# Attention scores on half the rows of the array, the two heads in turn

## The chip, the core and the metric

The kernel runs on one core of a Trainium2 chip. The metric is the device time of the whole launch in microseconds (us), the median of several runs. The core's engines work side by side and each runs its own instructions in order: TensorE (PE; PEld in rows is its loading of weights), VectorE (DVE), ScalarE (ACT), GpSimd (POOL). SyncE (SP) issues the transfers (DMA) from and to memory. SBUF is the large memory on the chip with 128 partitions (rows); PSUM, in eight banks, is where TensorE writes.

## The reference, cut to what matters

```python
def _attn_ref(q, k, v, M_prev, z_prev, beta):          # B, H, S, D = 4, 8, 576, 64
    scores = q @ k^T / sqrt(D);  causal mask
    a = softmax(scores)
    local = a @ v
    q_p = where(q > 0, q, exp(q) - 1) + 1
    mem_out = (q_p @ M_prev) / (q_p . z_prev + 1e-6)
    g = sigmoid(beta)
    return g * mem_out + (1 - g) * local
# then, on the 2304 tokens with 512 channels:
#   h = x @ w_in; solu = h * softmax(h); layer norm * g_ln; @ w_out
#   sigmoid(x @ w_gate) * (x @ w_val) @ w_out
```

There are 32 heads (4 batches of 8) of 576 positions and 64 channels. The scores are causal, so a query needs only the keys up to its own position.

## The kernel before, in words

The program has three parts: attention, the first expert layer (`Moe1`) and the gated second one (`Moe2`). Only attention is changed.

Attention takes the heads in 16 pairs. A pair's q, k and features are transposed on TensorE (`trans`, line 265; tiles trq, trk, trf), so that channels lie on the partitions: head 0 on rows 0 to 63, head 1 on rows 64 to 127. For accuracy q and k are each split into a high and a low part (`tq_h`, `tq_l`, `tk_h`, `tk_l`: ScalarE writes the high part, VectorE the low one); a score is the sum of three products, q high by k high, q low by k high, q high by k low. Queries go in blocks of 128 (blocks 0 to 3) and a tail of 64 (block 4, where both heads' tails share the 128 columns of the weights and the 576 keys are cut in two halves). Block i needs 128 (i + 1) keys.

In `s_p` (line 352) q is the stationary operand and k the moving one. Both heads' k lie in one tile of 128 rows, so q is kept in a tile `q2` that has zeros in the rows of the other head: head 0's columns first, then the tails, then head 1's. GpSimd writes these zeros once at the start (line 185). Each matmul uses all 128 rows; the first head's three are issued, then the second's.

VectorE adds the mask and takes the row maxima (`s_m`, line 372), ScalarE the exponentials and their sums (`s_e`, line 380), GpSimd divides (`n_p`, line 389). The probabilities are transposed (`g_p`, `t_p`, `tt_p`, `tc_p`: tiles t..a, t..b, t..c, t..d) and copied to SBUF by ScalarE or VectorE. The products with v and with the memory (`x_m` line 444, `x_a` line 459; tile x) are f32 matmuls with 64 columns of weights, head 0 on the left columns of the array and head 1 on the right ones; each leaves two records in the trace. The share of the memory is computed beside it (`ph_e` to `ph_s`). In the gaps the first layer's weights are converted (`cv_*`).

Scores and the three transposes of q, k and features take turns in two PSUM buffers of two banks each (tag "s"); the transposed probabilities have two buffers of one bank, x two.

The order of all this is a table, `ORDER`: each entry names a step and the pair it works on, as an offset to the running index. `run` walks the table once per index, so it fixes the order on every engine. The steps around attention, among them the load gl (line 794) and its scaling on VectorE (line 795), are placed by a planner.

Of the kernel before, what the change touches and what calls it, by code (L numbers as in the profile page):

```python
# [9 lines left out]
F32R = mybir.dt.float32r  # L10
# [8 lines left out]


ORDER = """
n23_r:-1 s1_e:0 s4_m:0 tt_c:-1 tc_c:-1 s3_m:0 lk:1 cv_r:-1 n3_p:-1 s0_e:0 s4_e:0 x1_c:-2 a00:-2 g1_p:-1 tf_p:0
t3_p:-1 g1_c:-1 tf_c:0 n2_p:-1 t3_c:-1 x0_c:-2 s2_p:0 t2_p:-1 t0_p:-1 cv_b:-1 ph_e:1 t2_c:-1 n4_r:0 n01_r:0 tq_p:1
cv_p:-1 n1_p:0 lz:1 t0_c:-1 t1_p:-1 g0_p:-1 cv_h:-1 tq_h:1 s2_m:0 t1_c:-1 ph_m:1 tk_p:1 tk_h:1 x0_m:-1 x1_m:-1
a13:-1 tq_l:1 tk_l:1 ph_g:1 n0_p:0 n4_p:0 cv_d:1 lv:0 a12:-1 a11:-1 a14:-1 a10:-1 ph_r:1 lq:2 ph_s:1 s3_e:0 s2_e:0
a01:-1 s1_p:1 s0_p:1 s1_m:1 tt_p:0 s0_m:1 g0_c:-1 tc_p:0 s4_p:1 cv_l:-1 s3_p:1 cv_a:0
""".split()


# [6 lines left out]
def f32(ap):  # L36
    return ap.bitcast(F32)
# [13 lines left out]
def kernel(  # L51
# [16 lines left out]
    nc = tc.nc  # L68
    B, H, S, D = q.shape
# [3 lines left out]
    P = 128  # L73
    NB = S // P
    S0 = NB * P
    TL = S - S0
# [74 lines left out]
    class Attention:  # L151
        def __init__(self, sb, ps, xe):
            self.sb, self.ps = sb, ps
            hw = S // 2

            self.pr = [{} for _ in pairs]
            self.kt = [xe.tile([P, 10 * D], F32, tag="xs", name=f"kt{n}") for n in range(2)]
            self.zm = sb.tile([P, HP, P], F32, tag="zm", name="zm0", bufs=2)
            self.qt = [sb.tile([P, 10 * D], F32, tag=f"qt{n}", name=f"qt{n}") for n in range(2)]


            mask = sb.tile([P, 2 * S0], F32, tag="mask", name="mask")
            nc.gpsimd.memset(mask, 0.0)
            for m in (mask[:, S0 - P : S0], *(mask[r : r + 64, S0 + hw - TL : S0 + hw] for r in (0, 64))):
                nc.gpsimd.affine_select(
                    out=m, in_=m, pattern=[[-1, m.shape[1]]], compare_op=ALU.is_ge,
                    fill=-1e30, base=0, channel_multiplier=1,
                )
            self.mask = mask[:, :S0]
            self.maskt = mask.rearrange("p (j w) -> p j w", j=2)[:, :, :hw]  # L170


            tail = slice(8 * D, 10 * D)
            self.vt = [sb.tile([P, 10 * D], F32, tag=f"vt{n}", name=f"vt{n}") for n in range(3)]
            for t in (*self.kt, *self.qt, *self.vt):
                nc.vector.memset(t[64:128, tail], 0.0)
            self.p4, self.q2 = [], []
            for n in range(2):
                p4 = sb.tile([P, S + TL], F32, tag=f"p4{n}", name=f"p4{n}")
                nc.vector.memset(p4[:, S:], 0.0)  # L180
                self.p4.append(p4)

                q2 = sb.tile([P, 2, 2 * S], F32R, tag=f"q2{n}", name=f"q2{n}")
                for hh in range(2):
                    nc.gpsimd.memset(f32(q2[64 - 64 * hh : 128 - 64 * hh, :, hh * S : hh * S + S]), 0.0)
                self.q2.append(q2)
            self.mt = []
            for n in range(3):
                mt = sb.tile([P, 2, D], F32, tag=f"mt{n}", name=f"mt{n}")
                nc.vector.memset(mt, 0.0)  # L190
                self.mt.append(mt)
# [29 lines left out]
            return self.ps.tile(shape, F32, tag=tag, name=name, bufs=2)  # L221


        def load_qk(self, n, t, src):
            b, hp = pairs[n]
            for hh in range(2):
                nc.sync.dma_start(
                    t[:, : 8 * D].rearrange("p (c h d) -> p c h d", h=2, d=D)[:, :, hh],
                    src[b, 2 * hp + hh, :S0, :].rearrange("(c p) d -> p c d", p=P),
                )  # L230
            nc.sync.dma_start(
                t[0:64, 8 * D : 10 * D].rearrange("p (h d) -> p h d", h=2),
                src[b, 2 * hp : 2 * hp + 2, S0:, :].rearrange("h p d -> p h d"),
            )
# [2 lines left out]
            self.load_qk(n, self.qt[n % 2], q)  # L237

        def lk(self, n, r):
            self.load_qk(n, self.kt[n % 2], k)  # L240

        def lv(self, n, r):
            b, hp = pairs[n]
# [27 lines left out]

        def q_parts(self, n, r):

            for hh, src, dst in ((0, 0, 0), (1, 0, S + TL), (1, S0, S)):
                sl, w = slice(64 * hh, 64 * hh + 64), S if hh == 0 else S0 if src == 0 else TL
                yield r["qps"][sl, src : src + w], *(self.q2[n % 2][sl, c, dst : dst + w] for c in range(2))

        def tq_h(self, n, r):
# [59 lines left out]
        def s_p(self, n, r, i):  # L338
            ps = r["s", i] = self.psum([P, 2, 512], f"sc{n}_{i}")
            q2, kh, kl = self.q2[n % 2], r["kh"], r["kl"]  # L340
            for j in range(2):
                if i == NB:

                    ks, x = slice(j * S // 2, (j + 1) * S // 2), ps[:, j, : S // 2]
                    qs = [q2[:, c, S0 : S0 + P] for c in range(2)]
                else:
                    w = P * (i + 1)
                    ks, x = slice(0, w), ps[:, j, :w]
                    q0 = w - P + j * (S + TL)
                    qs = [q2[:, c, q0 : q0 + P] for c in range(2)]  # L350
                for m, (c, kk) in enumerate(((0, kh), (1, kh), (0, kl))):
                    nc.tensor.matmul(x, qs[c], kk[:, ks], start=m == 0, stop=m == 2)  # L352

        def parts(self, r, i):

# [444 lines left out]
    ps = ctx.enter_context(tc.tile_pool(name="ps", bufs=2, space=PSUM, reuse_waits="tile"))  # L800
# [51 lines left out]
```

## Time and profile before

| | us |
|---|---|
| median of three runs (915.29 to 916.43) | 916.21 |
| the profiled execution | 914.82 |
| its span, first to last instruction | 913.0 |
| TensorE busy | 888.3 (97%) |
| VectorE busy | 567.2 (62%) |
| ScalarE busy | 432.1 (47%) |
| GpSimd busy | 267.0 (29%) |

The busy shares are means over stages that differ. Attention fills the first 238 us and there VectorE and ScalarE are nearly as busy as TensorE; in the layers that follow TensorE alone is. A row of the list of instructions gives line, engine, operation, written tile <- read tiles, shapes, count, and busy time with the mean in ns. In the list by time the first number is the start, the second how long the group took; TensorE's instructions are pipelined, so their cost is read from start to start and not from the durations. An idle time before a group stands in brackets with what ended it.

### The profile page before, as it was taken

The page shows a single profiled execution, that of the slowest core. Times are in us where ns is not written, and L with a number is a line of the kernel's source. Part 1 is how long each engine was busy: PE and PEld are TensorE (multiplying, and loading weights), DVE is VectorE, ACT ScalarE, POOL GpSimd, SP SyncE. Part 2 cuts the span into 40 slices and gives each one's busy share as a digit, 9 for nine tenths or more (in the row PEclk, how much of TensorE's full clock was granted, in tenths as well). Part 3 has the DMA queues.
Part 4 walks back from the last instruction along what each step waited for, and adds up shares of the span by engine and source line. Part 5 has one row for each costly group of instructions (what it writes and reads, how often), then busy time and mean ns, then how long its engine had stood idle before and what let it go on. Part 6 is the DMA issues. An engine that isn't in the chain of part 4 may idle for free.

```text
span 913.0 us, 13960 instructions
## 1 busy us (share of the span) xinstructions
PE 888.3 (97%) x5224; PEld 753.2 (82%) x5224; DVE 567.2 (62%) x1321; ACT 432.1 (47%) x941; POOL 267.0 (29%) x322
## 2 busy tenths in 40 slices
PE   5899999999989999999999999999999999999998
PEld 4788788787778998999998888888888888888887
DVE  5899999999587655664825158366349735232324
ACT  3799999998577455464535333112122212111111
POOL 4566665666565211112400034021014103000000
PEclk9899999999999999999999999999999999999999
DMA  5243533443122100110300013012003200000113
GB/s 127 51 94 81 115 90 89 97 104 88 47 70 71 47 24 24 36 58 24 116 1 1 1 53 109 23 27 67 1 1 106 79 0 1 1 1 1 47 46 116
DMA packets 76291, 48.62 MB, mean 53 GB/s; under 512 B 62656, under 2 KB 62656, under 8 KB 76224
## 3 DMA queue, kind: packets, MB, share of 16 engines
q1 hardware_dynamic: 76224, 47.74, 19.1%
q8 instruction: 41, 0.67, 0.3%
q14 instruction: 26, 0.21, 0.1%
HBM read 43.00 MB, written 4.72 MB: 52 GB/s over the span
## 4 chain that ended last, share of the span: by engine, by line
PE 87%; DVE 7%; POOL 2%; ACT 1%; issue 1%; DMA 1%; SPq 1%; DVEq 0%; POOLq 0%; ACTq 0%
PE gv L730 32%; PE po L749 16%; PE po L648 9%; PE sc L352 8%; PE h L597 7%; PE x L459 5%; PE x L444 2%; PE pl L636 1%; PE trq L265 1%; DVE p L372 1%; PE trk L265 1%; PE trf L265 1%; DVE exwo L109 1%; DVE exwo L108 0%; DVE exwo L119 0%
## 5 line engine op out<-in xcount | busy, mean ns | idle before, releaser
L736 DVE TENSOR_TENSOR sg<-sg,gv 128x512 f32<-128x512 f32 (+1 forms) x60 | 38.0, 633 | 176.5 <-ACT sg L735 176.5
L735 ACT ACTIVATE sg<-gv 128x512 f32<-128x512 f32 (+1 forms) x60 | 33.1, 552 | 233.7 <-PE gv L730 233.7
L730 PE MATMUL gv<-xx,gh 128*128 128x512 f32 (+1 forms) x480 | 136.2, 368 | 0.2 <-ACT xx L138 0.2
L730 PE MATMUL gv<-xx,vh 128*128 128x512 f32 (+1 forms) x480 | 136.1, 368 | 0.0
L648 PE MATMUL po<-lnT,woh 128*128 128x256 f32 x576 | 104.9, 284 | 1.1 <-ACT woh L575 0.7
L730 PEld LDWEIGHTS gv<-xx,gh 128*128 128x128 f32 x480 | 87.4, 189 | 16.1 <-issue 0.4
L730 PEld LDWEIGHTS gv<-xx,vh 128*128 128x128 f32 x480 | 87.1, 189 | 15.0
L648 PEld LDWEIGHTS po<-lnT,woh 128*128 128x128 f32 x576 | 90.5, 192 | 2.7 <-ACT woh L575 0.9
L389 POOL TENSOR_SCALAR p<-p,rs 128x256 f32<-128x256 f32 (+2 forms) x144 | 78.3, 561 | 36.4 <-ACT ex L112 16.4
L380 ACT ACTIVATE p<-p,nm 128x256 f32<-128x256 f32 (+2 forms) x144 | 82.7, 579 | 12.6 <-DVE nm L372 12.6
L730 PE MATMUL gv<-xx,vl 128*128 128x512 f32 (+1 forms) x240 | 88.4, 368 | 0.0
L730 PE MATMUL gv<-xx,gl 128*128 128x512 f32 (+1 forms) x240 | 88.3, 368 | 0.0
L352 PE MATMUL sc<-kh,q 128*128 128x256 f32 (+4 forms) x320 | 79.5, 340 | 9.0 <-DVE nm L372 5.4
L597 PE MATMUL h<-wih,xs 128*128 128x512 f32 x288 | 81.5, 396 | 2.9 <-DVE e L610 2.9
L749 PE MATMUL po<-oh,GVxs 128*128 128x512 f32 x216 | 84.2, 390 | 0.0
L749 PE MATMUL po<-ol,GVxs 128*128 128x512 f32 x216 | 84.2, 390 | 0.0
L749 PE MATMUL po<-oh,GVe 128*128 128x512 f32 x216 | 84.1, 389 | 0.0
L648 PE MATMUL po<-lnT,wol 128*128 128x256 f32 x288 | 81.5, 284 | 1.1 <-POOL wol L145 1.1
L756 DVE TENSOR_TENSOR X<-X,po 128x512 f32<-128x512 f32 x90 | 61.3, 683 | 22.7 <-PE po L749 22.7
L352 PEld LDWEIGHTS sc<-kh,q 128*128 128x128 f32 x320 | 54.2, 200 | 14.6 <-DVE nm L372 6.5
L597 PEld LDWEIGHTS h<-wih,xs 128*128 128x128 f32 x288 | 53.2, 189 | 14.0 <-ACT e L619 2.9
L372 DVE CUSTOM_DVE_ANT_0 p<-sc,mask 128x256 f32<-128x256 f32 (+3 forms) x128 | 55.9, 483 | 9.9 <-PE sc L352 9.9
(351 smaller groups left out, 1785.0 us busy)
## 6 DMA issues: line engine op xcount, KB each, us to landing
rawg<-in_moe_w_gate_dram SPq DMA_DIRECT2D x12, 512.0 KB, 3.9
rawv<-in_moe_w_val_dram SPq DMA_DIRECT2D x12, 512.0 KB, 3.9
rawo<-in_moe_w_out_dram SPq DMA_DIRECT2D x12, 512.0 KB, 3.5
out_dram<-X SPq DMA_DIRECT2D x18, 256.0 KB, 2.0
qt<-in_q_dram SPq DMA_DIRECT2D x32, 128.0 KB, 2.7
kt<-in_k_dram SPq DMA_DIRECT2D x32, 128.0 KB, 2.8
raw<-in_moe_w_in_dram SPq DMA_DIRECT2D x16, 256.0 KB, 3.4
vt<-in_v_dram SPq DMA_DIRECT2D x32, 128.0 KB, 3.6
```

The costliest lines, as they stand in the source:

```text
L352: nc.tensor.matmul(x, qs[c], kk[:, ks], start=m == 0, stop=m == 2)
L372: nc.vector.tensor_tensor_reduce(p, x, m, -1.0, 3.0e38, ALU.add, ALU.min, nm)
L380: nc.scalar.activation(p, p, AF.Exp, bias=nm, scale=-1.0, accum_out=r["sum"][:, c : c + 1])
L389: nc.gpsimd.tensor_scalar(p, p, r["rs"][:, c : c + 1], 1.0, ALU.mult, ALU.mult)
L459: nc.tensor.matmul(r["x", g][64 * hh : 64 * hh + 64, c0 : c0 + src.shape[1]], r["vt"][:, c : c + D], src, start=False, stop=j == 0,)
L597: nc.tensor.matmul(ph[:, j * 512 : j * 512 + 512], xs[:, s, c], w[:, j * 512 : j * 512 + 512], start=(c == 0 and s == 0 and w is hi), stop ...
L648: nc.tensor.matmul(po[:, :GW], w[:, m * P : m * P + P], L[:, x, c], start=(c == 0 and n == 0), stop=(c == NF1 - 1 and n == 2),)
L730: nc.tensor.matmul(ps[:, j, :w], wt[:, c, fs], xx[:, x, c], start=(c == 0 and n == 0), stop=(c == NC - 1 and n == 2),)
L735: nc.scalar.activation(sg[:, :w], ps[:, 0, :w], AF.Sigmoid)
L736: nc.vector.tensor_mul(sg[:, :w], sg[:, :w], ps[:, 1, :w])
L749: nc.tensor.matmul(po, GV[x][:, f, sl], wt[:, f], start=(f == 0 and n == 0), stop=(f == NCH - 1 and n == 2),)
L756: nc.vector.tensor_add(acc[:, t], acc[:, t], po)
```

## The change

Blocks 0 to 3 of the scores use, for each head, only the 64 rows on which that head's channels lie, and within a term the two heads follow each other. The tile `q2` needs no zero rows for them any more: both heads share its first 512 columns, each on its own rows. Only the tails (block 4) keep zeros, in 128 columns. `q_parts` therefore writes one piece of 512 columns on 128 rows and two of 64. The first pair's k is loaded through ScalarE's queue. `ORDER` is a new table.

```diff
 ORDER = """
-n23_r:-1 s1_e:0 s4_m:0 tt_c:-1 tc_c:-1 s3_m:0 lk:1 cv_r:-1 n3_p:-1 s0_e:0 s4_e:0 x1_c:-2 a00:-2 g1_p:-1 tf_p:0
...
+s4_m:0 n3_p:-1 tq_p:1 ph_e:1 tf_c:0 tc_c:-1 g1_c:-1 t3_p:-1 s4_e:0 n2_p:-1 cv_l:-2 t0_p:-1 ph_m:1 t3_c:-1 t0_c:-1
...
-                q2 = sb.tile([P, 2, 2 * S], F32R, tag=f"q2{n}", name=f"q2{n}")
-                for hh in range(2):
-                    nc.gpsimd.memset(f32(q2[64 - 64 * hh : 128 - 64 * hh, :, hh * S : hh * S + S]), 0.0)
+                q2 = sb.tile([P, 2, S + TL], F32R, tag=f"q2{n}", name=f"q2{n}")
+                nc.gpsimd.memset(f32(q2[:, :, S0:]), 0.0)
...
-        def load_qk(self, n, t, src):
+        def load_qk(self, n, t, src, dma=nc.sync.dma_start):
...
-            self.load_qk(n, self.kt[n % 2], k)
+
+            self.load_qk(n, self.kt[n % 2], k, nc.sync.dma_start if n else nc.scalar.dma_start)
...
-            for hh, src, dst in ((0, 0, 0), (1, 0, S + TL), (1, S0, S)):
-                sl, w = slice(64 * hh, 64 * hh + 64), S if hh == 0 else S0 if src == 0 else TL
+            h0, h1 = slice(0, 64), slice(64, 128)
+            for sl, src, dst, w in ((slice(0, P), 0, 0, S0), (h0, S0, S0, TL), (h1, S0, S, TL)):
                 yield r["qps"][sl, src : src + w], *(self.q2[n % 2][sl, c, dst : dst + w] for c in range(2))
...
-            for j in range(2):
-                if i == NB:
-
-                    ks, x = slice(j * S // 2, (j + 1) * S // 2), ps[:, j, : S // 2]
-                    qs = [q2[:, c, S0 : S0 + P] for c in range(2)]
-                else:
-                    w = P * (i + 1)
-                    ks, x = slice(0, w), ps[:, j, :w]
-                    q0 = w - P + j * (S + TL)
-                    qs = [q2[:, c, q0 : q0 + P] for c in range(2)]
-                for m, (c, kk) in enumerate(((0, kh), (1, kh), (0, kl))):
-                    nc.tensor.matmul(x, qs[c], kk[:, ks], start=m == 0, stop=m == 2)
+            terms = ((0, kh), (1, kh), (0, kl))
...
+            w = P * (i + 1)
+            for m, (c, kk) in enumerate(terms):
+                for hh in range(2):
+                    sl = slice(64 * hh, 64 * hh + 64)
+                    nc.tensor.matmul(
+                        ps[:, hh, :w], q2[sl, c, w - P : w], kk[sl, :w], start=m == 0, stop=m == 2
+                    )
```

TensorE's queue in the steady rounds, first before. The names are tiles with the pair's number: sc4_1 is pair 4's block 1, kh and kl the high and low part of k, q2 the tile of q (its two copies are q20 and q21), x2_0 the output of pair 2's first 256 queries, A, Bt, C its transposed probabilities, t3c the transposed tail of pair 3.

```order
L459 MATMUL x2_0_919<-A2_843,vt2_107 64x128 x2
L352 MATMUL sc4_1_966<-kh4_917,q20_117 128x256 x2
L352 MATMUL sc4_1_966<-kl4_930,q20_117 128x256
L352 MATMUL sc4_1_966<-kh4_917,q20_117 128x256 x2
L352 MATMUL sc4_1_966<-kl4_930,q20_117 128x256
L352 MATMUL sc4_0_973<-kh4_917,q20_117 128x128 x2
L352 MATMUL sc4_0_973<-kl4_930,q20_117 128x128
L352 MATMUL sc4_0_973<-kh4_917,q20_117 128x128 x2
L352 MATMUL sc4_0_973<-kl4_930,q20_117 128x128
L425 MATMUL t3c_985<-ident_58,p41_120 128x128 x4
L432 MATMUL t3d_996<-ident_58,p41_120 128x128
L352 MATMUL sc4_4_998<-kh4_917,q20_117 128x288 x2
```

The same place in the changed program:

```order
L465 MATMUL x4_1_1360<-Bt4_1256,vt1_106 64x320 x6
L356 MATMUL sc6_0_1373<-kh6_1334,q20_117 128x128 x4
L356 MATMUL sc6_0_1373<-kl6_1343,q20_117 128x128 x2
L356 MATMUL sc6_1_1384<-kh6_1334,q20_117 128x256 x4
L356 MATMUL sc6_1_1384<-kl6_1343,q20_117 128x256 x2
L356 MATMUL sc6_2_1418<-kh6_1334,q20_117 128x384 x4
L356 MATMUL sc6_2_1418<-kl6_1343,q20_117 128x384 x2
L356 MATMUL sc6_3_1427<-kh6_1334,q20_117 128x512 x4
L356 MATMUL sc6_3_1427<-kl6_1343,q20_117 128x512 x2
L404 MATMUL t5a0_1434<-ident_58,p5_0_1186 128x128
L404 MATMUL t5a0_1434<-ident_58,p5_1_1200 128x128
L404 MATMUL t5a0_1434<-ident_58,p5_0_1186 128x128
```

Before, only blocks 1 and 0 stood behind x; blocks 4 and 3 came after the tail's transposes, then a piece of x, and block 2 after further transposes. Now blocks 0 to 3 stand in one stretch behind the whole of x, and block 4 comes after transposes.

SP's queue from the start to the load gl, before (eleven transfers stand ahead of these rows, bt, which is beta, as the fourth of them); qt, kt, vt are loads of q, k, v, mt of the memory, zm of z, raw of the first layer's weights:

```order
L231 DMA qt1_93<-in_q_dram 64x2x64
L227 DMA kt1_90<-in_k_dram 128x4x64 x2
L231 DMA kt1_90<-in_k_dram 64x2x64
L104 DMA raw1_312<-in_moe_w_in_dram 128x512
L227 DMA vt0_105<-in_v_dram 128x4x64 x2
L231 DMA vt0_105<-in_v_dram 64x2x64
L247 DMA mt0_125<-in_M_prev_dram 64x64 x2
L227 DMA qt0_92<-in_q_dram 128x4x64 x2
L231 DMA qt0_92<-in_q_dram 64x2x64
L227 DMA kt0_89<-in_k_dram 128x4x64 x2
L231 DMA kt0_89<-in_k_dram 64x2x64
L794 DMA gl_82<-in_moe_g_ln_dram 128x8x1
```

And in the changed program, behind the three loads of the first q:

```order
L254 DMA zm0_91<-in_z_prev_dram 128x512
L226 DMA qt1_93<-in_q_dram 128x4x64 x2
L230 DMA qt1_93<-in_q_dram 64x2x64
L226 DMA kt1_90<-in_k_dram 128x4x64 x2
L230 DMA kt1_90<-in_k_dram 64x2x64
L194 DMA bt_144<-in_beta_dram 128x8
L226 DMA qt0_92<-in_q_dram 128x4x64 x2
L230 DMA qt0_92<-in_q_dram 64x2x64
L226 DMA kt0_89<-in_k_dram 128x4x64 x2
L230 DMA kt0_89<-in_k_dram 64x2x64
L800 DMA gl_82<-in_moe_g_ln_dram 128x8x1
```

The load gl moves from the 28th transfer to the 18th, and bt from the fourth to the eleventh. On VectorE the scaling of gl stood between the first pair's blocks 4 and 3; now it stands in the middle of the gates' arithmetic, ahead of all of the first pair's reductions. On ScalarE the exponential of bt stands, as before, ahead of the first pair's q.

## Rows read from the trace of the kernel before

**Rows 1.** Busy time and count per engine of one round (PE, PEld, DVE, ACT, POOL)

```profile
103.97:117.26 13.29, 13.29 (x108) 10.80 (x107) 12.42 (x42) 12.49 (x35) 8.38 (x13) 1.00 0.48 110
```

**Rows 2.** Chain of waits over nine rounds, shares by line

```profile
by line: PE sc L352 35.9%; PE x L459 21.5%; PE x L444 8.4%; PE trk L265 4.1%; PE trq L265 4.1%; PE trf L265 4.1%; PE t4b L411 1.3%; PE t7b L411 1.3%; PE t8b L411 1.3%; PE t9b L411 1.3%; PE t10b L411 1.3%; PE t3b L411 1.3%; PE t6b L411 1.3%;
```

**Rows 3.** TensorE in order of time in that round: start, length, engine, instruction

```profile
105.40 0.71 PE L265 MATMUL trk<-ident,kt 128*128 128x128 f32 x5
106.04 1.19 PE L444 MATMUL x<-f,mt 128*64 128x256 f32 x8
...
108.58 0.71 PE L459 MATMUL x<-Bt,vt 128*64 128x320 f32 x4
109.12 0.39 PE L459 MATMUL x<-A,vt 128*64 128x128 f32 x4
109.44 0.50 PE L352 MATMUL sc<-kh,q 128*128 128x256 f32 x2
...
110.25 0.33 PE L352 MATMUL sc<-kh,q 128*128 128x128 f32 x2
...
110.86 0.62 PE L425 MATMUL t6c<-ident,p 128*128 128x128 f32 x4
...
112.24 0.63 PE L352 MATMUL sc<-kh,q 128*128 128x512 f32 x2
...
113.73 0.65 PE L459 MATMUL x<-A,vt 128*64 128x256 f32 x4
...
114.59 0.71 PE L265 MATMUL trf<-ident,E 128*128 128x128 f32 x5
115.13 0.38 PE L411 MATMUL t6b<-ident,p 128*128 128x128 f32 x2
115.27 0.59 PE L352 MATMUL sc<-kh,q 128*128 128x384 f32 x2
...
116.40 1.04 PE L411 MATMUL t6b<-ident,p 128*128 128x128 f32 x8
```

**Rows 4.** Groups by shape, nine rounds: count, busy us, mean ns, idle before

```profile
L280 ACT ACTIVATE q<-trq 64x576 fp32r<-64x576 f32 x9 | 5.8, 647 | 0.0
L280 ACT ACTIVATE q<-trq 64x512 fp32r<-64x512 f32 x9 | 5.3, 593 | 0.1
L280 ACT ACTIVATE q<-trq 64x64 fp32r<-64x64 f32 x9 | 1.9, 207 | 0.0
L284 DVE SCALAR_TENSOR_TENSOR q<-trq,q 64x576 fp32r<-64x576 f32 x9 | 6.7, 742 | 0.0
L284 DVE SCALAR_TENSOR_TENSOR q<-trq,q 64x512 fp32r<-64x512 f32 x9 | 6.3, 695 | 0.1
L284 DVE SCALAR_TENSOR_TENSOR q<-trq,q 64x64 fp32r<-64x64 f32 x9 | 2.0, 220 | 0.0
```

**Rows 5.** The start on VectorE, SP and TensorE; the page's group of reductions

```profile
11.51 0.20 DVE L206 RECIPROCAL bt<-bt 128x8 f32<-128x8 f32 x1
...
14.26 0.36 DVE L372 CUSTOM_DVE_ANT_0 p<-sc,mask 128x256 f32<-128x256 f32 x1
...
20.19 0.17 DVE L795 TENSOR_SCALAR gl<-gl 128x8 f32<-128x8 f32 x1 [2.56 <-DMA gl<-in_moe_g_ln_dram]
...
24.51 0.49 DVE L306 TENSOR_SCALAR E<-E 128x640 f32<-128x640 f32 x1
...
2.53 0.58 SPq L195 DMA_DIRECT2D bt<-in_beta_dram  x1
...
17.60 0.59 SPq L794 DMA_DIRECT2D gl<-in_moe_g_ln_dram  x1
...
23.31 1.05 PE L265 MATMUL trq<-ident,qt 128*128 128x128 f32 x4
...
210.97 0.71 PE L265 MATMUL trq<-ident,qt 128*128 128x128 f32 x5
...
L372 DVE CUSTOM_DVE_ANT_0 p<-sc,mask 128x256 f32<-128x256 f32 (+3 forms) x128 | 55.9, 483 | 9.9 <-PE sc L352 9.9
```

More of the change, by code (lines that the diff above doesn't have):

```diff
@@ L21 @@
 ORDER = """
-n23_r:-1 s1_e:0 s4_m:0 tt_c:-1 tc_c:-1 s3_m:0 lk:1 cv_r:-1 n3_p:-1 s0_e:0 s4_e:0 x1_c:-2 a00:-2 g1_p:-1 tf_p:0
[L23 to L26, printed above, removed]
+s4_m:0 n3_p:-1 tq_p:1 ph_e:1 tf_c:0 tc_c:-1 g1_c:-1 t3_p:-1 s4_e:0 n2_p:-1 cv_l:-2 t0_p:-1 ph_m:1 t3_c:-1 t0_c:-1
+tk_p:1 cv_a:-1 tq_h:1 n01_r:0 ph_g:1 tq_l:1 t1_p:-1 tk_h:1 cv_r:-1 t2_p:-1 tk_l:1 t2_c:-1 n0_p:0 t1_c:-1 cv_b:-1
+n4_r:0 x0_m:-1 a01:-1 a00:-1 x1_m:-1 a14:-1 a13:-1 a12:-1 a11:-1 a10:-1 s0_p:1 s3_e:0 n1_p:0 s1_p:1 ph_r:1 s2_e:0
+cv_p:-1 n4_p:0 s0_m:1 lq:3 lv:0 cv_h:-1 s1_m:1 s2_p:1 n23_r:0 s3_p:1 g0_p:0 tt_p:0 lk:3 ph_s:1 s2_m:1 lz:3 cv_d:0
+s4_p:1 x1_c:-1 s0_e:1 s1_e:1 tt_c:0 g0_c:0 s3_m:1 tf_p:1 x0_c:-1 tc_p:0 g1_p:0
 """.split()
@@ L221, in psum @@
             return self.ps.tile(shape, F32, tag=tag, name=name, bufs=2)
-        def load_qk(self, n, t, src):
+        def load_qk(self, n, t, src, dma=nc.sync.dma_start):
             b, hp = pairs[n]
             for hh in range(2):
-                nc.sync.dma_start(
+                dma(
                     t[:, : 8 * D].rearrange("p (c h d) -> p c h d", h=2, d=D)[:, :, hh],
@@ L230, in load_qk @@
                 )
-            nc.sync.dma_start(
+            dma(
                 t[0:64, 8 * D : 10 * D].rearrange("p (h d) -> p h d", h=2),
@@ L340, in s_p @@
             q2, kh, kl = self.q2[n % 2], r["kh"], r["kl"]
-            for j in range(2):
-                if i == NB:
-                    ks, x = slice(j * S // 2, (j + 1) * S // 2), ps[:, j, : S // 2]
-                    qs = [q2[:, c, S0 : S0 + P] for c in range(2)]
-                else:
-                    w = P * (i + 1)
-                    ks, x = slice(0, w), ps[:, j, :w]
-                    q0 = w - P + j * (S + TL)
-                    qs = [q2[:, c, q0 : q0 + P] for c in range(2)]
-                for m, (c, kk) in enumerate(((0, kh), (1, kh), (0, kl))):
-                    nc.tensor.matmul(x, qs[c], kk[:, ks], start=m == 0, stop=m == 2)
+            terms = ((0, kh), (1, kh), (0, kl))
+            if i == NB:
+                for j in range(2):
+                    ks = slice(j * S // 2, (j + 1) * S // 2)
+                    for m, (c, kk) in enumerate(terms):
+                        nc.tensor.matmul(
+                            ps[:, j, : S // 2], q2[:, c, S0:], kk[:, ks], start=m == 0, stop=m == 2
+                        )
+                return
+            w = P * (i + 1)
+            for m, (c, kk) in enumerate(terms):
+                for hh in range(2):
+                    sl = slice(64 * hh, 64 * hh + 64)
+                    nc.tensor.matmul(
+                        ps[:, hh, :w], q2[sl, c, w - P : w], kk[sl, :w], start=m == 0, stop=m == 2
+                    )
         def parts(self, r, i):
```

## The prediction

> **What bounds the kernel now.** I read the busy times of one round first, then the chain of waits, then TensorE's instructions in order of time, and last VectorE and ScalarE beside them. Attention works through 16 pairs of heads in a software pipeline; a round of it takes 13.29 us [rows 1]. TensorE is busy for all of it, VectorE for 12.42, ScalarE for 12.49, GpSimd for 8.38. The chain agrees: for nine rounds it is TensorE alone, and 35.9% of it are the score matmuls [rows 2]. So TensorE sets the round, and whatever is taken from it counts, but only until ScalarE or VectorE is full: they have 0.8 and 0.87 us left. From the transpose of the second pair's q (23.31) to that of the last (210.97) go 187.66 us [rows 5], 14 rounds of 13.40 in the mean; the first and last ones are longer than the steady 13.29. The experts' layers that follow keep their matmuls and their number; I count nothing there but a shift.
>
> **The change part by part.**
>
> *Scores.* Per pair and query block there are six matmuls (two heads, three terms). Start to start, six of 128 keys take 0.61 us, of 256 keys 0.81, of 384 keys 1.13, and of 512 keys 1.49 with a change of array shape at their end [rows 3]. Such a change costs 0.10: five transposes at 105.40 take 0.54 (as the five at 114.59 do), so they are through at 105.94, and the first x matmul starts at 106.04 [rows 3]. Without it the 512 are 1.39, and blocks 0 to 3 take 0.61 + 0.81 + 1.13 + 1.39 = 3.94 us of each round. After the change these 24 matmuls use 64 rows of the array each, head 0 the upper half and head 1 the lower, one after the other, into two different banks of PSUM. No row shows such a pair. Its cost lies between that of one full-height matmul (both at once: 1.97 a round) and that of two and a drain each (worked out under the rivals). The nearest rows are the x matmuls, which use half of the columns: four records of 320 take 108.58 to 109.12, 0.135 each, where a full-size score lies between 0.135 (256) and 0.19 (384); four of 128 take 0.22 without the change of shape that follows, 0.055 each, where an f32 transpose of 128 columns on the whole array takes 0.108 [rows 3]. Against wide score matmuls that is little gain, against their own kind (f32) it is a factor of two. I take the factor of two, because narrow records at 0.055 are faster than any full-size one in this trace, so half-array matmuls do go side by side here: 1.97 us less.
>
> The Trainium skill ("TensorE: Matmul & The Clock Gate", Part 3 on row and column tiling) says that matmuls whose operands lie in different row groups run together, a few ns apart. By it the 24 would take the 1.97 that I take; no run here shows row groups, and the x records speak for it only by way of columns.
>
> If the two heads' weights are loaded one after the other, a pair can't be quicker than twice the 0.10 that a 128-key matmul takes: 3 x (0.20 + 0.20 + 0.20 + 0.23) = 2.5, a gain of 1.4.
>
> *Order.* Blocks 0 to 3 now stand together, behind all of x; x has one stretch and no longer two. So a round has three changes of shape in place of four: 0.10 less. TensorE's round becomes 13.29 - 1.97 - 0.10 = 11.22 (11.8 with loads in turn). What is late next: all scores and the three transposes of q, k and features go through the same two PSUM buffers, so block 2 waits until VectorE has read block 0, block 3 for block 1. These reductions take some 3.5 us a pair (55.9 us in 16 pairs, the long row of [rows 5]), more than the 1.97 of matmuls that feed them, so part of the gain comes back as a wait here: 0.3 to 0.5, and TensorE's round is 11.6.
>
> *q without zero rows.* ScalarE writes q's upper halves in pieces of 512, 64 and 64 columns in place of 576, 512 and 64: 647 + 593 + 207 becomes 593 + 207 + 207, 0.44 less. VectorE: 742 + 695 + 220 becomes 695 + 220 + 220, 0.52 less [rows 4]. ScalarE's round is then 12.49 - 0.44 = 12.05 busy, VectorE's 11.90. These, not TensorE, are the new floor. Neighbours overlap a little inside the busy time, so the floor may lie some tenths lower; in-order engines that feed each other usually leave some tenths idle. I take 12.1 for the steady round, 1.19 less, and the same 1.19 for the irregular ones: 14 x 1.19 = 16.7 us.
>
> *Start.* VectorE waits 2.56 us for the small load gl, which SP issues at 17.60, its 28th transfer, and goes on at 20.19; the second pair's features begin at 24.51 [rows 5]. In the new order gl is the 18th transfer. It stands behind loads of q and k whose buffers the first pair's transposes have freed by then; ten issues of some 0.55 less bring it to about 12, and at VectorE 2.6 later, 14.5. But VectorE now meets it in the middle of the gates, with more work behind it: the rest of the gates and the features' sums (11.51 to 14.26, less 0.2: 2.5) and all reductions of the pair (4): 21, against 24.51. The gain is 3.5 at most; I take 3.0. One wait is new: beta's load goes from SP's fourth transfer (2.53) to its eleventh, some 4 us later, and on ScalarE the exponential of beta stands ahead of q's upper half. Queued behind it are that and k's; VectorE's q and TensorE's first scores wait for them. It costs 2 us there, which the wait for gl hides. Without that cover the start would gain 1 and not 3. The first load of k goes to ScalarE's queue, and the zeroing of q on GpSimd shrinks; both only touch the first 7 us, where the wait for gl covers them too.
>
> *End.* From 210.97 on the last pairs run out; the last scores are shorter, the copies are not: 0.7 less.
>
> Sum: 16.7 + 3.0 + 0.7 = 20.4. The profiled execution took 914.82 us, of which 913.0 is the span; 914.82 - 20.4 = 894.4. The median of the runs, 916.21, is 1.39 above the profiled one: 895.8, and I predict 896.
>
> Its own range: with a round of 11.6 (TensorE's own floor, if the busy time of ScalarE overstates it) another 14 x 0.5 = 7 go, 889, and a start that gains all of 3.5 makes it 888; with a round of 12.7 (loads in turn, waits at PSUM) 14 x 0.6 = 8.4 come back, and 2 more at the start: 906.
>
> **The rivals.**
>
> *The halves don't overlap.* Each part-height matmul then takes its 0.10 to 0.23 in turn, as now. For it: the x records of 320 at 0.135 each, little quicker than full-size ones. TensorE's round is 13.29 - 0.10 = 13.19, the savings on the other engines hide behind it, and what is left is 14 x 0.10 + 3.0 + 0.7 = 5.1: 911. If the start gains nothing, 914.
>
> *The halves disturb each other: slower.* If going from one half of the rows to the other drains the array as a change of shape does (0.10 [rows 3]), 24 such steps cost 2.4 a round on top of 3.94. The round becomes 13.19 + 2.4 = 15.6 and the whole 14 x 2.2 - 3.7 = 27 longer: 943. It turns slower than before once a step costs more than 5.1 / (14 x 24) = 0.015 us. Against it: a round now goes through such steps between column halves in x, where 320 columns cost 0.135 a record with no such gap. The Trainium skill ("TensorEngine Tiling (Array Packing)", Key Properties) says that changing the tiling mode drains the engine and changing the tile does not; the 0.10 in the rows agrees for the mode, and no row here shows the tile. By it this rival falls away, and I give it little.
>
> *The order eats the gain.* The halves overlap, but a round settles at 13.1, since t-copies of ScalarE now stand between q and k, and the next scores' exponentials wait behind the longest of them. 14 x 0.2 + 3.7 = 6.5: 910. For it: ScalarE would have 0.05 to spare at 12.1 and nearly every PSUM buffer waits on it.
>
> **How the numbers follow.** Forecast 0.66; no overlap 0.16; slower 0.12; order 0.06. A difference under 0.2% (1.8 us) can't be told from none here. Forecast is all faster. Of no overlap 0.11 is faster and 0.05 the same, with the start's gain lost. Order: 0.03 faster, 0.02 the same, 0.01 slower. Slower: 0.12. Together faster 0.80, same 0.07, slower 0.13. Range: from 887, a little under the forecast's own low end, to 913, which takes in most of the two cases at 910 and 911 and leaves out the slower one.
>
> **What would show it.** Right: blocks 0 to 3 in about 2 to 2.5 us of TensorE (3.94 now), with the two heads' matmuls starting within some ns of each other; rounds of 12 to 12.3; TensorE with idle time before scores, released by VectorE; ScalarE with under 0.3 idle; the second pair's q transpose at about 20 in place of 23.31; three changes of shape a round. Wrong: starts of the two heads that stand 0.10 to 0.23 apart and a round of 13.2 (no overlap) or 15 and more (drains); overlap and a round over 12.7 (order), with the waits on ScalarE's copies; or a stage after attention that is longer than before by as much as attention is shorter.

## The result, and the profile after

The changed kernel takes 921.18 us (median of 6 runs, 920.37 to 921.64) where the kernel before takes 915.19 on the same chip: a ratio of 1.0061, with a 95% interval of 1.0048 to 1.0074. It is slower by 0.6%; the prediction was 896, faster. The profiled execution took 921.52 us, against the 894.4 that the prediction's sum gave for one.

I look first at one round, as in [rows 1] (us, then busy time and count of PE, PEld, DVE, ACT, POOL):

```profile
103.94:117.38 13.44, 12.26 (x108) 8.90 (x108) 13.17 (x42) 11.97 (x35) 8.41 (x12) 1.00 0.39 91
```

TensorE has 1.2 us without work where it had none, and the round is 0.15 longer all the same. VectorE is busy for 13.17 of 13.44 us, though its work became less: 12.42 before. So either it got slower instructions, or busy does not mean working. TensorE in order of time, to be laid beside [rows 3]:

```profile
111.05 0.44 PE L356 MATMUL sc<-kh,q 64*128 64x128 f32 x4
111.32 0.27 PE L356 MATMUL sc<-kl,q 64*128 64x128 f32 x2
111.43 0.45 PE L356 MATMUL sc<-kh,q 64*128 64x256 f32 x4
111.72 0.28 PE L356 MATMUL sc<-kl,q 64*128 64x256 f32 x2
112.85 0.62 PE L356 MATMUL sc<-kh,q 64*128 64x384 f32 x4 [0.85 <-DVE nm L378]
113.31 0.34 PE L356 MATMUL sc<-kl,q 64*128 64x384 f32 x2
113.54 0.74 PE L356 MATMUL sc<-kh,q 64*128 64x512 f32 x4
114.11 0.40 PE L356 MATMUL sc<-kl,q 64*128 64x512 f32 x2
114.44 0.66 PE L404 MATMUL t6a<-ident,p 128*128 128x128 f32 x4
```

The blocks begin 0.38 (128 keys), 0.69 (384) and 0.90 us (512, with the change of shape) before what follows; with some 0.4 for 256 keys, the four take 2.3 us where they took 3.94. In the single records the two heads' matmuls start 3 to 4 ns apart. The third pair of a block starts 0.11 (128 keys), 0.12 (256), 0.17 to 0.18 (384) or 0.23 us (512) after the second, and the second 0.16 to 0.33 after the first. Two half-height matmuls run at about the price of one. The change does on TensorE what it was to do.

Where VectorE's time goes shows when its instructions are grouped by shape, over nine rounds (count | busy us, mean ns | idle before). In the kernel before:

```profile
L109 DVE TENSOR_SCALAR ex<-raw 128x256 int32<-128x256 int32 x9 | 2.6, 286 | 0.0
...
L322 DVE SCALAR_TENSOR_TENSOR nr<-nr,g 128x10 f32<-128x10 f32 x9 | 1.5, 170 | 0.3
```

and in the changed one:

```profile
L109 DVE TENSOR_SCALAR ex<-raw 128x256 int32<-128x256 int32 x9 | 15.0, 1668 | 0.0
...
L322 DVE SCALAR_TENSOR_TENSOR nr<-nr,g 128x10 f32<-128x10 f32 x9 | 5.4, 605 | 0.3
```

L109, the second instruction of the weights' conversion (step cv_a), handles the same 256 elements with the same operands in 1.67 us, not 0.29. L322 needs 0.60 for ten elements. What stands beside them is seen on both engines in order of time; first VectorE, then GpSimd:

```profile
105.99 0.28 DVE L108 TENSOR_SCALAR ex<-raw 128x256 int32<-128x256 int32 x1
106.19 1.67 DVE L109 TENSOR_SCALAR ex<-raw 128x256 int32<-128x256 int32 x1
107.78 0.15 DVE L390 SCALAR_TENSOR_TENSOR rs<-sum,o 128x4 f32<-128x4 f32 x1
...
111.58 0.60 DVE L322 SCALAR_TENSOR_TENSOR nr<-nr,g 128x10 f32<-128x10 f32 x1
...
113.40 0.48 DVE L390 SCALAR_TENSOR_TENSOR rs<-sum,o 128x4 f32<-128x4 f32 x1
```

```profile
106.16 1.56 POOL L311 TENSOR_TENSOR G<-E,zm 128x640 f32<-128x640 f32 x1 [2.83 <-DVE E L307]
...
111.42 0.75 POOL L395 TENSOR_SCALAR p<-p,rs 128x576 f32<-128x576 f32 x1
112.61 1.26 POOL L328 TENSOR_TENSOR E<-E,nr 128x640 f32<-128x640 f32 x1 [0.44 <-DVE nm L378]
```

L109 starts 0.03 us after GpSimd's product G and ends 0.15 after it (107.86 against 107.71). L322 ends with GpSimd's scaling of p (112.18 and 112.17). The second L390, 0.15 us when alone, ends with GpSimd's product E (113.89 and 113.87). Each time VectorE's instruction ends with GpSimd's or shortly behind it. I read this as a hold: VectorE stands until GpSimd's instruction is over, and the trace shows that as a long instruction and not as a wait. Against the 0.286 and 0.170 of the rows of before, and the 0.15 of an L390 alone, that is 1.38 + 0.43 + 0.33, some 2.15 us a round. The old order has cv_a at 112.02, where GpSimd is idle; the new one puts it right behind ph_m, whose end is what releases G. That gives theory 1: the new order lines VectorE's work up with GpSimd's, VectorE becomes the bound, and what TensorE saved is idle time there.

The Trainium skill ("SBUF — State Buffer", Who interferes with whom) says that the two engines share a pair of ports, which one of them locks for a whole instruction, and that VectorE wants it where an instruction has two inputs in SBUF or runs in a mode that uses two ports. The three holds agree with such a lock in where they end; L322 and L390 have two inputs, but that L109, with one, runs in a mode of two ports is shown by no row here. The prediction had not weighed this rule.

Theory 2, the rival, starts from the chain of waits, which names no line of VectorE (compare [rows 2]):

```profile
by line: ACT p L386 34.6%; POOL p L395 17.7%; ACT Bt L135 11.1%; ACT q L280 6.9%; ACT E L300 6.1%; issue 5.7%; ACT kh L135 4.8%; ACT f L135 3.9%; ACT ex L112 3.0%; ACT X L135 2.4%; ACT ex L491 2.3%; ACT wih L506 2.2%
```

By it a loop through ScalarE and the features' only buffer E sets the round: the exponential that fills E for the next pair (L300) waits for the transposes of E, and the copy of the features, the exponentials and x stand behind it.

### The profile page after: what moved, and what is told of

The parts are those of the page before. It is cut to its first block, busy times and chain, and to the rows that moved or that the text cites. A ratio compares the mean times of both kernels' runs of the same rounds, so it can differ in the third digit from the quotient of the medians.

```text
span 919.7 us, 13972 instructions
## 1 busy us (share of the span) xinstructions
PE 870.2 (95%) x5224; PEld 723.4 (79%) x5224; DVE 578.1 (63%) x1321; ACT 423.8 (46%) x941; POOL 260.1 (28%) x320
## 4 chain that ended last, share of the span: by engine, by line
PE 69%; ACT 15%; DVE 7%; POOL 5%; issue 3%; DMA 1%; SPq 0%; POOLq 0%; DVEq 0%; ACTq 0%
PE gv L736 32%; PE po L755 16%; PE po L654 9%; PE h L603 7%; ACT p L386 6%; POOL p L395 3%; ACT Bt L135 2%; ACT q L280 1%; PE pl L642 1%; ACT E L300 1%; ACT kh L135 1%; ACT f L135 1%; PE sc L356 1%; PE x L465 1%; DVE exwo L109 1%
## 5 line engine op out<-in xcount | busy, mean ns | idle before, releaser
L386 ACT ACTIVATE p<-p,nm 128x128 f32<-128x128 f32 (+2 forms) x144 | 83.0, 585 | 7.0 <-DVE nm L378 7.0
L395 POOL TENSOR_SCALAR p<-p,rs 128x128 f32<-128x128 f32 (+2 forms) x144 | 78.5, 563 | 20.0 <-DVE rs L391 13.3
L356 PE MATMUL sc<-kh,q 64*128 64x128 f32 (+3 forms) x256 | 37.2, 376 | 25.2 <-DVE nm L378 17.9
L142 POOL TENSOR_SCALAR gh<-exg 128x512 fp32r<-128x512 f32 x12 | 8.9, 749 | 183.0 <-PE gv L736 142.1
L138 ACT CAST GVxs<-sg 128x512 fp32r<-128x512 f32 (+1 forms) x60 | 34.8, 580 | 46.5 <-DVE sg L742 46.5
```

Of the source, the lines that this page charges most:

```text
L138: nc.scalar.copy(hi, src)
L356: nc.tensor.matmul(ps[:, hh, :w], q2[sl, c, w - P : w], kk[sl, :w], start=m == 0, stop=m == 2)
L386: nc.scalar.activation(p, p, AF.Exp, bias=nm, scale=-1.0, accum_out=r["sum"][:, c : c + 1])
L395: nc.gpsimd.tensor_scalar(p, p, r["rs"][:, c : c + 1], 1.0, ALU.mult, ALU.mult)
```

## The experiments

**The two halves of the change apart.** The first kernel has the row halves and the new q under the table ORDER of before, with the old loads of k:

```diff
-            self.load_qk(n, self.kt[n % 2], k, nc.sync.dma_start if n else nc.scalar.dma_start)
+            self.load_qk(n, self.kt[n % 2], k, nc.sync.dma_start)
```

> Scores on row halves and q without zero rows, under the old order and with the old loads of k. Theory 1 (in the new order VectorE stands still while GpSimd works, 2.15 us a round: 1.39 in the second instruction of the weights' conversion, 0.43 and 0.33 in two small products): the old order has that conversion elsewhere, so the second instruction of it takes 0.29 us, not 1.67; a round takes 12.0 to 12.7 us in place of 13.29, and the kernel 896 to 906 us. Theory 2 (the halves themselves can't shorten a round, since the loop through the features' single buffer E and the PSUM slots sets it): the round stays at 13.2 to 13.5 us, the time at 912 to 918.

Measured: 902.91 us, ratio 0.9866 (0.9852 to 0.9879). The round is 12.64 us, and L109 takes 0.287. As theory 1 expected; theory 2 as it stands there falls.

```profile
96.83:109.47 12.64, 12.51 (x109) 9.06 (x107) 12.27 (x42) 11.89 (x35) 8.37 (x13) 1.00 0.50 115
```

The second has the old scores and the old q under the new ORDER; the first k's load stays the new one:

```diff
-                    nc.tensor.matmul(
-                        ps[:, hh, :w], q2[sl, c, w - P : w], kk[sl, :w], start=m == 0, stop=m == 2
-                    )
+                    q0 = w - P + j * (S + TL)
+                    qs = [q2[:, c, q0 : q0 + P] for c in range(2)]
...
+                    nc.tensor.matmul(x, qs[c], kk[:, ks], start=m == 0, stop=m == 2)
```

> The old scores (zero rows, full height) and the old q under the new order. Theory 1: VectorE's held time stays (second conversion instruction at 1.5 us or more) and its q work is 0.52 longer, so the round is 13.7 to 14.2 us, over the 13.29 that TensorE needs, and the kernel takes 925 to 935 us. If the new order is innocent, TensorE bounds as before: 13.2 to 13.5, 914 to 920 us.

Measured: 939.48 us, ratio 1.0270 (1.0256 to 1.0284); the round is 14.64 us, L109 takes 1.66. The direction is theory 1's; the size is missed: the round by 0.44 us, the kernel by 4.5. My sum took the longer of TensorE's and VectorE's time. Here VectorE is busy for 13.90 of 14.64 us and TensorE for 13.98, and the chain of waits goes through the old scores (23.8%), VectorE's held product on ten elements (4.2%, L323 in that kernel) and ScalarE in turn, so the two seem to wait for each other in part; no run tried it.

The row halves alone gain 11.8 us, the new order alone costs 24.8, and both together cost 6 to 6.5; so under the new order the halves are worth some 18. The slowdown is the order's (with it goes the first k's load on ScalarE's queue, which was not tried apart). In the old order with row halves the chain of a round runs mostly through VectorE (busy for 12.27 of 12.64), and it is still held there: L322 for 0.55 us, one L390 for 0.65.

**Away from the product G.** Two steps of VectorE move ahead of ph_m.

```diff
-... cv_l:-2 t0_p:-1 ph_m:1 t3_c:-1 t0_c:-1 tk_p:1 cv_a:-1 tq_h:1 n01_r:0 ph_g:1 ...
+... cv_l:-2 t0_p:-1 cv_a:-1 n01_r:0 ph_m:1 t3_c:-1 t0_c:-1 tk_p:1 tq_h:1 ph_g:1 ...
```

> The changed kernel with one stretch of VectorE's order moved: the first step of the weights' conversion and the first reciprocals stand ahead of the features' min and max, not behind them, so not beside GpSimd's product G. Theory 1: the second conversion instruction takes 0.29 us, the two other held ones stay; the round is 12.0 to 12.5 us in place of 13.45, the kernel 902 to 908 us. Theory 2 (loop through E and PSUM slots): G now starts 0.8 later, the round stays at 13.3 to 14.2 us, the kernel at 919 us or more.

Measured: 914.80 us, ratio 1.0003 (0.9993 to 1.0013), 6.4 less than the changed kernel in place of 13 to 19. L109 takes 0.288 us, as theory 1 said. But the rounds are uneven, 12.70 to 14.07. One reason is a new wait, of VectorE for a load of the weights, in ten rounds (us in total, times, longest):

```profile
DVE ex L108 <- DMA raw<-in_moe_w_in_dram: 8.0, 7, 2.4
```

Moved half a round earlier, cv_a meets its load before it has landed. And other instructions now meet GpSimd: one L390 is held in seven of the ten rounds, for up to 1.19 us, each time until GpSimd's product E (L328) or a scaling ends. This run shows L109's hold gone, not what it was worth.

**The same place, without G.** This tells a hold by GpSimd from a slow place on VectorE.

```diff
-            r["G"] = self.sb.tile([P, 10 * D], F32, tag="G", name=f"G{n}")
-            nc.gpsimd.tensor_mul(
-...
+            r["G"] = r["E"]
```

> The changed kernel with the product of the features and z on GpSimd left out (the sums are taken of the features themselves); everything else stands where it stood. Theory 1 (GpSimd's work holds VectorE's second conversion instruction): that instruction falls from 1.67 to 0.29 us in the same place, the round from 13.45 to 12.1-12.7, the kernel to 903-911 us. If the instruction is slow because of what precedes it on VectorE, it stays at 1.6 and so does the round: 919 to 922 us.

Measured: 910.73 us, ratio 0.9958 (0.9941 to 0.9974). L109 stands where it stood, right behind L307 and L108, and is short; L317 (L322 of the changed kernel) still meets a scaling on GpSimd and stays held:

```profile
102.59 0.30 DVE L108 TENSOR_SCALAR ex<-raw 128x256 int32<-128x256 int32 x1
102.81 0.30 DVE L109 TENSOR_SCALAR ex<-raw 128x256 int32<-128x256 int32 x1
...
107.42 0.61 DVE L317 SCALAR_TENSOR_TENSOR nr<-nr,g 128x10 f32<-128x10 f32 x1
```

So it is GpSimd's work that holds it. The time is no clean price of the hold, since GpSimd too is rid of 1.56 us a round; the next run keeps G. The round is 12.86 us, a little over the 12.7 that theory 1 allowed: something else stops it there.

**The large holds away.** cv_a, n01_r and n4_r ahead of ph_m, n23_r behind s2_m, on GpSimd n4_p ahead of cv_p, and the raw weights one round earlier.

```diff
-... cv_l:-2 t0_p:-1 ph_m:1 ... cv_a:-1 ... n01_r:0 ... n4_r:0 ... cv_p:-1 n4_p:0 ... n23_r:0 ... s2_m:1 ... cv_d:0
+... cv_l:-2 t0_p:-1 cv_a:-1 n01_r:0 n4_r:0 ph_m:1 ... n4_p:0 cv_p:-1 ... s2_m:1 n23_r:0 ... cv_d:1
```

> The changed kernel with VectorE's held instructions moved off GpSimd's work: the first conversion step and two groups of reciprocals ahead of the features' min and max, the third group behind the 384-key scores, on GpSimd the last block's scaling ahead of the conversion product; and the raw weights loaded one round earlier, since in the run with the conversion moved VectorE waited for them up to 2.3 us. Theory 1: no instruction of VectorE is held for over 0.3 us, the round is 12.0 to 12.5 us even (ScalarE's 12.0 to 12.1 busy is next), the kernel 901 to 908 us. Theory 2 (something else in the new order sets the round, such as PSUM slots): still 12.9 us or more, 912 or more.

Measured: 911.45 us, ratio 0.9968 (0.9956 to 0.9979). L109 takes 0.285 us, L322 0.32, each group of reciprocals 0.16; VectorE is busy for 11.8 of a round of 12.76, no longer full. The large holds are gone; some 0.15 stay at L322 and 0.13 at L117. The kernel is 9.7 us faster than the changed one, but the round is 0.26 and the kernel 3.5 us above what theory 1 expected; the result lies between the two theories' ranges.

```profile
113.94:126.72 12.78, 12.27 (x109) 8.91 (x107) 11.79 (x42) 11.96 (x35) 8.73 (x13) 1.00 0.46 104
```

TensorE and ScalarE at its end:

```profile
125.80 0.74 PE L265 MATMUL trf<-ident,E 128*128 128x128 f32 x5
```

```profile
125.51 0.58 ACT L135 COPY A<-t7a 128x512 f32<-128x512 f32 x1
126.62 0.74 ACT L300 ACTIVATE E<-qt 128x640 f32<-128x640 f32 x1 [0.53 <-POOL p L395]
127.27 0.62 ACT L135 COPY f<-trf 128x576 f32<-128x576 f32 x1
```

The row names GpSimd's p as what released L300. But the instruction that fills E has to wait for the transposes that read it, and these run from 125.80 to 126.54; L300 starts at 126.62. Behind it on ScalarE are queued the copy of the features, the last block's exponentials and a copy of probabilities, and only behind these come TensorE's next transposes and x. This looks like theory 2's loop; the second of the next two runs tests it.

**Two buffers for E**, once in the changed kernel and once in the one without the large holds.

```diff
-            r["E"] = self.sb.tile([P, 10 * D], F32, tag="E", name=f"E{n}")
+            r["E"] = self.sb.tile([P, 10 * D], F32, tag="E", name=f"E{n}", bufs=2)
```

> The changed kernel with two buffers for the features E in place of one, so that ScalarE's exp needn't wait for the transposes of the pair before. Theory 2 (the loop through E sets the round): the round falls to 12.7 us or less, the kernel to 911 us or less. Theory 1: ScalarE starts exp earlier, but VectorE is busy 13.1 of 13.4 us and nothing moves: 13.3 to 13.5, 919 to 922 us.

Measured: 922.76 us, ratio 1.0087 (1.0073 to 1.0101), 0.8 above theory 1's range; rounds of 13.44 us, but for one of 14.91 and the last of 15.65. Alone it brings nothing: theory 1.

> The kernel with VectorE's held instructions moved, with two buffers for the features E. In that kernel the rounds of 12.76 us close through E: ScalarE's exp of the next pair waits until TensorE has transposed E (0.5 us a round), and the feature copy, the last block's exp and TensorE's x stand behind it. If that loop is the second thing behind the held work, the round falls to 12.0-12.5 us and the kernel from 911.5 to 902-908 us. If not (PSUM slots or ScalarE's work alone), it stays at 12.7 and 909 to 913.

Measured: 904.49 us, ratio 0.9893 (0.9878 to 0.9908). Two rounds:

```profile
110.74:123.06 12.32, 12.10 (x108) 8.89 (x106) 11.62 (x42) 11.99 (x36) 8.65 (x13) 1.00 0.41 98
123.06:135.33 12.27, 12.03 (x109) 9.01 (x107) 11.73 (x42) 11.75 (x35) 8.77 (x13) 1.00 0.42 99
```

12.28 us in the mean, and the chain of such a round is TensorE again, but for two short stays at VectorE's reductions. So both theories were true, one behind the other: the holds set 13.44 us, the loop through E 12.76, TensorE with its waits some 12.3.

**The load of beta.** To that kernel:

```diff
-                if it == -1:
+                if it == -2:
                     self.gates_load()
```

> The same, with the small load of beta issued before the loads of the second pair, not behind them. ScalarE's exp of beta stood 2.5 us waiting for it, with q of the first pair behind. If that wait costs the start what it delays, the first scores come 2 to 2.6 us earlier and the kernel is 1.5 to 2.6 us faster than without; if the start is bound by the features and gates behind them, under 0.8 us.

Measured: 900.93 us, ratio 0.9853 (0.9836 to 0.9869), 3.6 less. The first scores come at 10.21 us and not at 13.20, the second pair's q at 20.9 and not at 24.1. The start is bound by this wait, which is worth 3.2 us there; the other 0.4 lie in the first expert layer. I had expected up to 2.6 in all.

**Reciprocals in the old order.** Row halves and the old order, with n01_r and n4_r ahead of cv_b, so that they do not meet cv_p on GpSimd.

```diff
-... cv_b:-1 ph_e:1 t2_c:-1 n4_r:0 n01_r:0 tq_p:1 ...
+... n01_r:0 n4_r:0 cv_b:-1 ph_e:1 t2_c:-1 tq_p:1 ...
```

> Row halves under the old order, with two groups of reciprocals moved ahead of the second conversion step on VectorE, so that none stands beside GpSimd's conversion product, where one was held 0.50 us. Theory 1: VectorE's 12.27 busy falls by 0.5, the round from 12.64 to 12.1-12.3, the kernel from 902.9 to 895-898 us. If TensorE's waits or ScalarE set the round there, it stays at 12.5 to 12.7 and the kernel at 901 to 904.

Measured: 900.31 us, ratio 0.9841 (0.9822 to 0.9859); the round is 12.42 us, above the 12.1 to 12.3 of theory 1 and below the 12.5 of the other. The held L390 went from 0.65 to 0.15, but L306, L307 and the conversion's last subtraction now meet GpSimd and are 0.13, 0.15 and 0.06 us longer than before that move, so about half of the expected gain came. This kernel and the one with beta's early load beat both the kernel before and the changed one, by 1.5% and 2.2%.

**Heads not in turn.** Row halves and the old order, with the three terms of one head ahead of those of the other.

```diff
-            for m, (c, kk) in enumerate(terms):
-                for hh in range(2):
+            for hh in range(2):
+                for m, (c, kk) in enumerate(terms):
```

> Row halves under the old order, but the three terms of one head first and then the three of the other, not the heads in turn. If the heads overlap only where neighbours lie on different row halves, one meeting in five is left: blocks 0 to 3 cost about 3.3 us a round in place of 2.2, so the round is 13.0 to 13.5 us and the kernel 908 to 914. If TensorE runs the halves side by side whatever their order, nothing changes: 12.6, 902 to 904 us.

Measured: 903.81 us, ratio 0.9881 (0.9862 to 0.9899), rounds of 12.66: no change. In the program's order such a block reads kh, kh, kl of one head and then kh, kh, kl of the other. The rows of the trace have another one in every block of the steady rounds, all four of kh first:

```profile
96.86 0.62 PE L356 MATMUL sc<-kh,q 64*128 64x384 f32 x4
97.32 0.34 PE L356 MATMUL sc<-kl,q 64*128 64x384 f32 x2
97.59 0.33 PE L417 MATMUL t5b<-ident,p 128*128 128x128 f32 x1
```

The single records start 10 to 14 ns apart in pairs (96.862 and 96.872, 97.141 and 97.155), and the block takes 0.73 us, as it does in turn (107.79 to 108.51, 0.72, in the first experiment). TensorE starts the other head's first matmul although the first head's three stand ahead of it, two of which have not begun. Taking the heads in turn was not needed.

## Why the prediction was wrong

27.1 us lie between the predicted 894.4 and the 921.5 of the profiled execution. The 14 rounds from the second pair's q to the last pair's take 189.0 us (23.50 to 212.50) where 171.0 were predicted: 18.0. The second pair's q comes 0.2 us later than before and not 3.0 earlier: 3.2. From the last pair's q to the experts' first matmul it takes 31.3 us (212.50 to 243.83) where it took 27.4 and I had counted 0.7 less: 4.6. The first expert layer takes 1.2 more. The rest is the same to 0.1.

- *Scores: right.* Row halves run at once; 1.7 of the 1.97 us came. The rivals without overlap and with drains fall. (In the sum of the one with drains, 13.19 + 2.4 is 2.3 and not 2.2 above the steady round, so it should have come to 945 and not 943.)
- *One change of shape less, and TensorE's wait at PSUM: right in kind, too small.* Blocks 0 and 2 share a buffer; TensorE waits 0.85 us between them in the changed kernel, more than the 0.3 to 0.5 that I took. I put TensorE's own round at 11.6. Where TensorE sets it (the run without the large holds and with two buffers for E) it is 12.28, of which some 11.7 are matmuls, where I had 11.22, and 0.6 the wait.
- *q without zero rows: right.* The six groups of [rows 4] are now these, so 0.4 us less on ScalarE and 0.55 on VectorE:

```profile
L280 ACT ACTIVATE q<-trq 128x512 fp32r<-128x512 f32 x9 | 5.5, 615 | 0.0
L280 ACT ACTIVATE q<-trq 64x64 fp32r<-64x64 f32 x18 | 3.9, 217 | 0.1
...
L284 DVE SCALAR_TENSOR_TENSOR q<-trq,q 128x512 fp32r<-128x512 f32 x9 | 6.1, 676 | 0.0
L284 DVE SCALAR_TENSOR_TENSOR q<-trq,q 64x64 fp32r<-64x64 f32 x18 | 3.9, 217 | 0.1
```

- *"These, not TensorE, are the new floor ... I take 12.1 for the steady round": this is the step that failed.* I carried VectorE's busy time over from the old order as if it were a property of the instructions. It hangs on what GpSimd does at the same moment, and a new order changes just that. VectorE's floor was 13.2, not 11.9. My own evidence was in the trace: the old rounds had one L384 of 0.65 us in place of 0.15, which ends at 104.02 where GpSimd's product L496 (from 103.28) ends at 104.01, and I had not asked why:

```profile
103.38 0.65 DVE L384 SCALAR_TENSOR_TENSOR rs<-sum,o 128x4 f32<-128x4 f32 x1
```

  Behind it the loop through E would have stopped the round at 12.76, which I had not seen either: E has one buffer, and no row of before shows the wait, since TensorE was the bound. With both out of the way the round comes to 12.28, near my 12.1, but that is luck: TensorE sets it, and not ScalarE and VectorE, as I had it.
- *The order eats the gain: the right rival, with the wrong mechanism and too little chance (0.06).* I had put it down to ScalarE's copies. ScalarE is idle for 1.5 us of the round.
- *Start: wrong.* gl came earlier as predicted, and VectorE waits 1.23 us for it in place of 2.56 [rows 5]. But beta's wait stands on ScalarE ahead of q, and it is not hidden. And ScalarE's first exponential starts 1.7 us later, because q's first load lands later; first the row of before, then the changed kernel's:

```profile
5.42 0.74 ACT L300 ACTIVATE E<-qt 128x640 f32<-128x640 f32 x1
```

```profile
7.15 0.74 ACT L300 ACTIVATE E<-qt 128x640 f32<-128x640 f32 x1
10.42 0.21 ACT L302 ACTIVATE bt<-bt 128x8 f32<-128x8 f32 x1 [2.53 <-DMA bt<-in_beta_dram]
10.53 0.93 ACT L280 ACTIVATE q<-trq 128x512 fp32r<-128x512 f32 x3
...
12.69 0.69 PE L356 MATMUL sc<-kh,q 64*128 64x128 f32 x4 [5.28 <-DVE q L284]
...
23.50 0.77 PE L265 MATMUL trq<-ident,qt 128*128 128x128 f32 x5 [0.18 <-DVE nm L378]
```

  I had said that without the cover the start gains 1; the run with the early load shows the wait worth 3.2 at the start, so the cover that I named did not exist. In that run the second pair's q comes 2.4 us earlier than before (20.92), not far from the 3.0. What delays q's first load was not tried: the first k, loaded through the other queue, now comes in beside it. In the old order with the old loads that exponential starts at 5.49.
- *End: wrong.* In the run-out the changed kernel takes 3.9 us more than the one before. With the large holds moved away it takes 29.1 in place of 31.3, with the second buffer and beta's early load 28.9; so 2.2 of the 3.9 go with the holds, and the rest stays open. The 1.2 us in the first expert layer come with the new order (1.0 with the old scores, 0.1 with the halves in the old order); their cause was not tried and stays open.

## What to carry to other kernels

An engine's busy time is no floor for a new order while a neighbour can hold it up: before moving work, list which of VectorE's instructions slow down beside GpSimd's, and see which will stand side by side in the new order. A bound that the profile names hides those behind it; here three lay within 1.2 us of a round, and taking away the second before the first gained nothing. Time an edit and a new order apart: the first gained 1.3% and the second lost 2.7%.

## What the runs showed of the hardware

- Some of VectorE's instructions last until the GpSimd instruction beside them ends: 0.29 becomes 1.67 us beside one of 1.56, an operation on ten elements 0.60 in place of 0.17, one on four up to 1.19 in place of 0.15. Its instructions that read PSUM (q, kl, the scores' reductions) and the sum of G (0.76 to 0.82) were not lengthened. The trace shows the hold as busy time.
- fp32r matmuls on two row halves start 3 to 4 ns apart in the changed kernel (10 to 14 in the block shown of the run that does not take the heads in turn), and TensorE pairs them out of the program's order, past two matmuls that have not begun. So what was said of the core at the start, that each engine runs its instructions in order, does not hold for these. The Trainium skill ("TensorE: Matmul & The Clock Gate", The mechanism, in Part 3) has the few ns, and the trace agrees; it also has matmuls start strictly in the program's order, and there the last experiment shows otherwise.
